# Four of a pair's seven Strassen products in one accumulator, with the partial sums and phi's linear part on ScalarE

## The chip, the cores and the metric

The kernel runs on one core of a Trainium2 chip. The metric is device microseconds of one execution. A core has five engines that run at the same time, each with its own queue of instructions in order: TensorE (PE, matmuls, with weight loads PEld beside it), VectorE (DVE), ScalarE (ACT), GpSimd (POOL) and SyncE (SP, here a queue that issues transfers). Sums of matmuls are formed in PSUM banks of 128x512 fp32; everything else lies in SBUF.

## What is computed

The reference is one transformer block with adaLN conditioning, 2048 rows of 512. Cut to what matters:

```python
phi = lambda t: jnp.where(t > 0, t + 1, jnp.exp(t)) + 1e-6
pq, pk = phi(q), phi(k)                       # 32 heads of 16
kv  = jnp.einsum("bhsd,bhse->bhde", pk, v)
z   = jnp.einsum("bhsd->bhd", pk)
num = jnp.einsum("bhqd,bhde->bhqe", pq, kv)
den = jnp.einsum("bhqd,bhd->bhq", pq, z)[..., None] + 1e-6
o   = num / den                               # then @ wo, gate, residual
...
h   = jnp.einsum("bsd,df->bsf", x, w1) + b1   # x: the normed, modulated rows; 512 -> 1792
act = h * jnp.tanh(softplus(h))               # Mish
y   = jnp.einsum("bsf,fd->bsd", act, w2)      # 1792 -> 512, gate, residual
```

## The kernel before

**Products of fp32 quality.** Every operand is split into a high half (rounded to fp32r) and a low half (what is left). `split` (L71) does this: the high half by a copy on ACT, then, one tick later, the low half by a subtraction on DVE. A product of two split operands is three matmuls (`mm3`, L65): high by high, high by low, low by high. So the third matmul of a group stands on the low half of the operand that is split last.

**Order of the work.** The schedule is written by hand: each engine runs its instructions in the order in which the code emits them. A unit of PE's work is emitted, then work that follows from it is put on a list (`spawn`), and each `tick` lets every generator on the list emit its next step on DVE, ACT or POOL. An instruction whose input isn't ready holds all that is behind it on its engine.

**Stages.** Four blocks of 512 rows go through the layer norm, transposes, then K (`k_unit`, `k_post`), V's part of the sums (`g_unit`), then Q (`q_unit`), the denominators (`den`, L668 on) and the output projection (`o_unit`). `phi` (L239) reads the product in PSUM: Exp on ACT, then on DVE min(e, 1) + 1e-6 and max(p, 0) + that (L243, L244). phi(K) of the four blocks is added into block 0's tiles by DVE (L253) and summed over rows by `z_unit`.

**The feed-forward by Strassen and Winograd.** The first matrix product is taken in 2x2 blocks: a pair g of two column groups of the weights (a11, a12, a22 and sums s1 to s4 of them) and two blocks of rows (b11, b12, b21, b22 and differences t1 to t4). Seven products of 6 matmuls of 128x512 (`product`, L911) and some adds give the four blocks of the result, c11, c12, c21 and c22, each followed by bias and Mish on ACT. There are 7 pairs (G = 7), and all this is done twice: first for row blocks 0 and 1 (loop from L1012), then for blocks 2 and 3 (L1133 on), in the order of pairs 5, 6, 0, 1, 2, 3, 4.

- `pair_begin` (L924): the product a11 b11 and its copy u1 by ACT (L927). The first two pairs are begun early.
- `pair_unit` (L935): s2 t2 is added to u1 on DVE (u2), s3 t3 to that (u3), s1 t1 to u3 (c22), a22 t4 to u3 (all by `add`, L922), a12 b21 is chained by PE onto the bank of a11 b11 (`pair_first`) and s4 b22 onto the bank of s1 t1; the latter with u2 gives c12.
- `mish` (L884) leaves a result that is split at once for the second matrix product; `mish_b` (L905) keeps it for later.
- `trail` and `d_unit` (L891): the second matrix product of one column group of the first row block, 12 matmuls of 128x512. In the first half two of these trailing units stand behind each pair, those of the pair before it. `norm_tile` puts the layer norm of later rows (row sums L210 and L211, apply L198) beside it, `rows` and `w2_job` put the preparation of the next pair's weights (L586 to L589, L513).
- `second` (L962) does the second product of block 1 after all seven pairs.
- In the last half the second matrix product is by Strassen too: `e_unit` does its products m1 and m2 of a pair (12 matmuls of 128x256 each), one pair late; m4, m6, m7, m5 and m3 follow when all pairs are done. `left_trail` prepares their operands on DVE (L1070 to L1074).

PSUM has three kinds of banks: 4 of "acc" (sums of the second product), 3 of "h" and 1 of "tp". SBUF tiles of 128x512 come from one ring of 101.

Of the kernel before, what the change touches and what calls it, by code (L numbers as in the profile page):

```python
# [13 lines left out]
P = 128  # L14
S = 2048
# [10 lines left out]
def block_kernel(ctx: ExitStack, tc: tile.TileContext, x, wqkv, wo, w1, b1t, w2, c, wmodt, out):  # L26
# [18 lines left out]
    def f32(t):  # L45
        return t.bitcast(F32)
# [21 lines left out]
        pe.matmul(o, st[0], mv[1], start=False, stop=False)  # L68
        pe.matmul(o, st[1], mv[0], start=False, stop=stop)  # L69

    def split(name, t, keep, key, lo_engine=dve, hi_engine=act):  # L71

        hi, lo = sb(f"{name}h", F32R, t.shape), sb(f"{name}l", F32R, t.shape)
        if hi_engine is act:
            act.activation(hi, t, AF.Copy)
        else:
            hi_engine.tensor_copy(hi, t)
        if lo_engine is dve:
            yield
        lo_engine.tensor_tensor(lo, t, f32(hi), op=ALU.subtract)  # L80
        keep[key] = hi, lo


# [153 lines left out]
    ku, pk, pq, qs, ms = {}, {}, {}, {}, {}  # L237

    def phi(p, name, dst):  # L239
        e = sb(f"e_{name}")  # L240
        act.activation(e, p, AF.Exp)  # L241
        yield
        dve.tensor_scalar(e, e, 1.0, TINY, op0=ALU.min, op1=ALU.add)  # L243
        dve.scalar_tensor_tensor(dst, p, 0.0, e, op0=ALU.max, op1=ALU.add)  # L244

    def k_post(p, b, t, hi_engine=act):
        u = ku[b, t] = sb(f"ku_{b}_{t}")
        yield from phi(p, f"k_{b}_{t}", u)
        yield from split(f"pk_{b}_{t}", u, pk, (b, t), hi_engine=hi_engine)
        if b:  # L250
            if b < NB - 1:
                yield
            dve.tensor_tensor(ku[0, t], ku[0, t], ku.pop((b, t)), op=ALU.add)  # L253

    def k_unit(b, t):
        p = ps("h", f"pk_{b}_{t}")
# [19 lines left out]
    def z_unit():  # L276

        p = ps("h", "z")
        for t in range(4):
            pe.matmul(p[32 * t:32 * (t + 1), :], ones[:, 0:32], ku.pop((0, t)), start=True, stop=True)  # L280
        act.activation(zsum[0], p, AF.Copy)
        dve.tensor_tensor(zsum[1], p, f32(zsum[0]), op=ALU.subtract)

    def q_unit(b, g):
        p = ps("h", f"pq_{b}_{g}")
# [188 lines left out]
            yield  # L474

    zc = cst.tile([P, 4], F32, name="zc")
    zs = {}

    def z_side():

        zbc_ps = ps("tp", "zbc")
        for i in range(2):
            pe.matmul(zbc_ps, w32, zsum[i], start=i == 0, stop=i == 1)
        zbc = sb("zbc_sb")
        act.activation(zbc, zbc_ps, AF.Copy)
        yield
        for g in range(4):
            diag = cst.tile([P, P], F32, tag="diag", name=f"diag_{g}", bufs=1)
            dve.scalar_tensor_tensor(diag, zbc[:, P * g:P * (g + 1)], 1.0, ident, op0=ALU.mult, op1=ALU.mult,
                                     accum_out=zc[:, g:g + 1])  # L490
            dve.tensor_scalar(hmask[:, g, :], hmask[:, g, :], zc[:, g:g + 1], 1.0, op0=ALU.mult, op1=ALU.mult)
        for k in range(4):
            zs[k] = sb(f"zs_{k}")
            dve.tensor_scalar(zs[k], zbc, mc[:, k:k + 1], 1.0, op0=ALU.mult, op1=ALU.mult)


    w2s, w2d, w2f, op_a = {}, {}, {}, {}
# [171 lines left out]
    def attend(b, wait, queue=pool):  # L669

        p = ps("tp", f"den_{b}")[:, 0:P]
        for g in range(4):
            for t in range(4):
                pe.matmul(p[32 * t:32 * (t + 1), :], hmask[:, g, :], pq[b, g][:, P * t:P * (t + 1)],
                          start=g == 0, stop=g == 3)
        yield
        rden = cst.tile([P, P], F32, tag="rden", name=f"rden_{b}", bufs=2)
        dve.tensor_scalar(rden, p, TINY, 1.0, op0=ALU.add, op1=ALU.mult)
# [101 lines left out]
    def columns(c0, c, done):  # L780

        b11, b12, b21, b22 = [hf.pop((b, c + h)) for h in (0, 2) for b in (c0, c0 + 1)]
        t = [sb(f"t_{c0}_{c}_{i}") for i in range(4)]
        for d, u, v in (t[0], b12, b11), (t[1], b22, t[0]), (t[2], b22, b12), (t[3], b21, t[1]):
            dve.tensor_tensor(d, u, v, op=ALU.subtract)
        yield
        names = [("b11", b11), ("t2", t[1]), ("t3", t[2]), ("t1", t[0]), ("b22", b22), ("t4", t[3]), ("b21", b21)]
# [133 lines left out]
    def add(out, p, u):  # L921
        dve.tensor_tensor(out, p, u, op=ALU.add)  # L922

    def pair_begin(g, tag):  # L924

        u1, p = sb(f"u1_{g}"), product(g, "a11", "b11", tag)
        act.activation(u1, p, AF.Copy)  # L927
        return u1, p

    def pair_first(c0, g, p):  # L930
        m = mish(product(g, "a12", "b21", onto=p), c0, 2 * g)
        next(m)
        spawn(m)

    def pair_unit(c0, g, u1=None, tags=("tp", "h")):  # L935

        f = 2 * g
        u2, u3, c12, c22 = [sb(f"{n}_{g}") for n in ("u2", "u3", "c12", "c22")]
        p11 = None
        if u1 is None:  # L940
            u1, p11 = pair_begin(g, tags[0])
        add(u2, product(g, "s2", "t2"), u1)
        add(u3, product(g, "s3", "t3", tags[1]), u2)
        tick()
        p = product(g, "s1", "t1")
        add(c22, p, u3)
        mish_b(c22, f + 1)
        add(u3, product(g, "a22", "t4"), u3)
        spawn(mish(u3, c0, f + 1))
        tick()  # L950
        if p11 is not None:
            pair_first(c0, g, p11)
        add(c12, product(g, "s4", "b22", onto=p), u2)
        mish_b(c12, f)
        tick()

    def prep_a(b, f):
# [35 lines left out]
            load_wb(6)  # L993


    begun = [pair_begin(g, "h") for g in range(2)]
    tick()
    for g in range(2):
        pair_first(0, g, begun[g][1])
        tick()  # L1000
    for t in (2, 3):
        o_unit(NB - 1, t, "h")
        tick()
    tiles = [norm_tile(b, t) for b in (2, 3) for t in range(4)]
    def trail(f):
        if tiles and (f == 0 or f % 2):
            spawn(tiles.pop(0))
        d_unit(0, f, f)
        ahead(1, f)
        tick()  # L1010

    for g in range(G + 1):  # L1012
        if g < G:
            for f in (2 * g, 2 * g + 1) if g else ():
                spawn(w2_job(f))
            if g == 0:
                spawn(rows(2, 3))
            if g and tiles:
                spawn(tiles.pop(0))
            pair_unit(0, g, begun[g][0] if g < 2 else None)  # L1020
            if g < G - 2:
                store_rows(g)
            if 0 < g < G - 2:
                spawn(rows(g + 2, 2))
            if g == G - 1:
                for n in range(8):
                    load_back("n", nd, 2 + n // 4, n % 4)
        for f in ((0,), (1,))[g] if g < 2 else (2 * g - 2, 2 * g - 1):
            trail(f)
    second(1, prepare)  # L1030


# [25 lines left out]
    def bank(name, i):  # L1058
        return banks[name][i].rearrange("p (t c) -> p t c", t=2)

    def e_unit(n):
        g = pairs[n]
        for c, name in enumerate(("m1", "m2")):
            seventh(name, "acc", ag[L, 2 * g + c], [w[:, c, :] for w in wb[g]], n, G - 1)

    def left_sums(g):

# [49 lines left out]
    def load_wt(name, g):  # L1117
# [10 lines left out]
        else:  # L1128
            pool.dma_start(v, w2t[g][:, :, SUM[name], :])  # L1129

    for n, g in enumerate(pairs):
        if n < 5:
            if n:  # L1133
# [6 lines left out]
        if n == 6:  # L1140
            for m in pairs[:5]:
                load_wt("m4", m)
        pair_unit(L, g, tags=("h", "tp") if n == 1 else ("tp", "h"))
        if n < EARLY:
            spawn(left_trail(g))
        if n:
            e_unit(n - 1)
            tick()

    names = ["m4", "m6", "m7", "m5", "m3"]  # L1150
    units = [(name, n) for name in names for n in range(G)]
# [5 lines left out]
    for k, (name, n) in enumerate(units[:4 * G]):  # L1157
# [12 lines left out]
            spawn(finish(name))  # L1170
        tick()
        if k == 1:
            e_unit(G - 1)
            spawn(finish("m2"))
            tick()

# [41 lines left out]
```

## Time and profile before

| | |
|---|---|
| median of 3 runs | 499.61 us (499.48 to 499.65) |
| the profiled execution | 499.56 us |
| its span, first to last instruction | 497.9 us |
| matmuls | 2648 |
| instructions of DVE, ACT, POOL | 730, 472, 238 |
| granted TensorE clock, mean | 1.000 |

The difference between the profiled execution and its span, 1.66 us, lies ahead of the first and behind the last instruction. In the page's rows, a group is "line, engine, operation, output<-inputs, shapes, count | busy us in all, mean ns of one | idle time ahead of them and what ended it"; a name without its number stands for all tiles of that kind. PE's matmuls overlap: one of 128x512 is listed with 0.39 us, but the next starts 0.23 us later. Products in the pairs appear with outputs `p_a` and `p_s` (L917), the trailing units as `oacc`, m1 to m7 as `m`.

### The profile page before, as it was taken

To read this page: it belongs to the slowest core of one execution; us is meant where nothing else is said; L and a number is where in the kernel's file an instruction comes from. 1 tells how busy PE (TensorE), PEld (TensorE's weight loads), DVE (VectorE), ACT (ScalarE), POOL (GpSimd) and SP (SyncE) were. 2 spreads that over 40 slices of the span, in tenths; PEclk is the share of its full clock that TensorE was granted. 3 is DMA by queue.
4 is the path that set the end of the run, shared out by engine and by line. 5 is a ranking of instruction groups with operands and counts; after the bars stand their busy time and mean duration, and the time that the engine had idled before them with its cause. 6 is when DMAs were issued, how large, how long until landed. Compare 5 with 4: busy or idle time off the path is not lost.

```text
span 497.9 us, 7665 instructions
## 1 busy us (share of the span) xinstructions
PE 490.8 (99%) x2648; PEld 412.3 (83%) x2648; DVE 377.5 (76%) x730; ACT 264.4 (53%) x472; POOL 137.2 (28%) x238
## 2 busy tenths in 40 slices
PE   7999999999999999999999999999999999999997
PEld 5778888878778888888878888888788888899997
DVE  6889775889997979966776765679876666688671
ACT  6776674533351979637787555187343444469000
POOL 4471000100212323101443312323455131545200
PEclk9999999999999999999999999999999999999999
DMA  8721413381554307497799965999999273789312
GB/s 309 284 84 44 156 34 107 127 276 43 131 150 129 96 27 254 142 344 241 245 332 377 289 185 167 307 356 329 376 326 276 63 191 84 188 195 269 91 43 86
DMA packets 65613, 96.49 MB, mean 194 GB/s; under 512 B 7277, under 2 KB 31733, under 8 KB 65574
## 3 DMA queue, kind: packets, MB, share of 16 engines
q1 hardware_dynamic: 37220, 52.51, 31.8%
q0 software_dynamic: 28208, 43.21, 31.2%
q8 instruction: 21, 0.34, 0.3%
q10 hardware_dynamic: 146, 0.26, 0.1%
q14 instruction: 18, 0.15, 0.1%
HBM read 62.92 MB, written 33.03 MB: 193 GB/s over the span
## 4 chain that ended last, share of the span: by engine, by line
PE 95%; DVE 2%; DMA 1%; ACT 1%; POOL 0%; issue 0%; ACTq 0%
PE p_s L917 15%; PE p_a L917 12%; PE oacc L69 5%; PE oacc L68 5%; PE oacc L67 5%; PE m L69 5%; PE m L68 5%; PE m L67 5%; PE o L67 3%; PE pq L67 3%; PE o L69 3%; PE o L68 3%; PE pq L69 3%; PE pq L68 3%; PE gacc L68 3%; PE gacc L69 3%
## 5 line engine op out<-in xcount | busy, mean ns | idle before, releaser
L909 ACT ACTIVATE ub<-c,b1c 128x512 f32<-128x512 f32 x28 | 20.2, 720 | 55.6 <-DVE c L922 55.0
L922 DVE TENSOR_TENSOR c<-p_s,u 128x512 f32<-128x512 f32 x28 | 19.3, 689 | 25.1 <-PE p_s L917 25.1
L922 DVE TENSOR_TENSOR u<-p_s,u 128x512 f32<-128x512 f32 x28 | 19.4, 692 | 22.0 <-PE p_s L917 15.7
L189 POOL TENSOR_TENSOR rs_n<-rs_n,half 128x1 f32<-128x1 f32 x16 | 10.0, 624 | 40.6 <-DVE rs_n L215 31.0
L1129 POOL DMA_DIRECT2D wt_m<-w2t x20 | 14.0, 702 | 24.6 <-PE p_a L917 11.8
L775 ACT ACTIVATE hf_n<-tp_n,mc 128x512 f32<-128x512 f32 x16 | 11.7, 771 | 16.6 <-PE tp_n L773 16.6
L241 ACT ACTIVATE e_q<-pq 128x512 f32<-128x512 f32 x16 | 9.4, 589 | 19.9 <-PE pq L69 19.9
L927 ACT ACTIVATE u<-p_a 128x512 f32<-128x512 f32 x14 | 8.3, 592 | 21.4 <-PE p_a L917 21.4
L241 ACT ACTIVATE e_k<-pk 128x512 f32<-128x512 f32 x16 | 9.4, 591 | 13.2 <-PE pk L69 13.0
L189 POOL TENSOR_TENSOR rs_x<-rs_x,half 128x1 f32<-128x1 f32 (+1 forms) x10 | 7.1, 717 | 33.0 <-DVE rs_x L184 32.2
L573 POOL DMA_DIRECT2D w2b<-w2d x20 | 10.7, 539 | 18.4 <-DVE a_1l L80 4.9
L243 DVE TENSOR_SCALAR e_k<-e_k 128x512 f32<-128x512 f32 x16 | 6.8, 428 | 10.1 <-ACT e_k L241 9.9
L922 DVE TENSOR_TENSOR u<-p_a,u 128x512 f32<-128x512 f32 x14 | 9.7, 692 | 6.0 <-PE p_a L917 5.3
L681 POOL DMA_DIRECT2D rden_d<-rden x3 | 2.2, 739 | 43.1 <-DVE rden L679 43.1
L198 ACT ACTIVATE x<-x,nb_x,rs_x 128x512 f32<-128x512 f32 x15 | 11.6, 807 | 4.5 <-DVE nb_x L193 3.3
L567 POOL DMA_DIRECT2D wb<-w2d x14 | 9.9, 709 | 11.8 <-PE p_a L917 9.3
L693 DVE TENSOR_TENSOR q<-q,rd 128x512 f32<-128x512 f32 x16 | 10.5, 686 | 2.7 <-DMA rd<-rden_d 2.7
L705 DVE TENSOR_TENSOR r<-o,r 128x512 f32<-128x512 f32 x16 | 10.8, 678 | 1.8 <-PE o L69 1.8
L244 DVE SCALAR_TENSOR_TENSOR ku<-pk,e_k 128x512 f32<-128x512 f32 x16 | 11.1, 692 | 0.7
L244 DVE SCALAR_TENSOR_TENSOR q<-pq,e_q 128x512 f32<-128x512 f32 x16 | 11.1, 692 | 0.7
L886 ACT ACTIVATE u<-u,b1c 128x512 f32<-128x512 f32 x14 | 10.0, 715 | 2.8 <-DVE u L922 2.6
L180 DVE BATCH_NORM_STATS2 st_x<-x 128x6 f32<-128x512 f32 x13 | 8.9, 683 | 3.0 <-DMA x<-in_x_dram 3.0
(1328 smaller groups left out, 1921.8 us busy)
## 6 DMA issues: line engine op xcount, KB each, us to landing
wm<-in_wmodt_dram SPq DMA_DIRECT2D x24, 256.0 KB, 5.0
w2b<-w2d POOLq DMA_DIRECT2D x20, 256.0 KB, 6.2
wt_m<-w2t POOLq DMA_DIRECT2D x20, 256.0 KB, 4.1
r<-in_x_dram SPq DMA_DIRECT2D x16, 256.0 KB, 2.8
x<-in_x_dram SPq DMA_DIRECT2D x15, 256.0 KB, 4.8
w1p<-in_w_dram SPq DMA_DIRECT2D x14, 256.0 KB, 4.4
w2r<-in_w_dram SPq DMA_DIRECT2D x14, 256.0 KB, 3.1
wb<-w2d POOLq DMA_DIRECT2D x14, 256.0 KB, 4.6
```

What stands on the lines that cost most here:

```text
L67: pe.matmul(o, st[0], mv[0], start=start, stop=False)
L68: pe.matmul(o, st[0], mv[1], start=False, stop=False)
L69: pe.matmul(o, st[1], mv[0], start=False, stop=stop)
L189: pool.tensor_tensor(y, y, half[:, lo:hi], op=ALU.pow)
L198: act.activation(dst, t, AF.Identity, bias=nb[key, b][:, j:j + 1], scale=rs[key, b][:, j:j + 1])
L241: act.activation(e, p, AF.Exp)
L244: dve.scalar_tensor_tensor(dst, p, 0.0, e, op0=ALU.max, op1=ALU.add)
L775: act.activation(hf[b, j], p, AF.Identity, bias=mc[:, 12 + j:13 + j], scale=mc[:, 16 + j:17 + j])
L909: act.activation(u, p, AF.Mish, bias=b1c[:, f:f + 1])
L917: pe.matmul(p, st, mv, start=onto is None and c == 0 and i == 0, stop=c == 1 and i == 2, skip_group_check=onto is not None)
L922: dve.tensor_tensor(out, p, u, op=ALU.add)
L1129: pool.dma_start(v, w2t[g][:, :, SUM[name], :])
```

## The change

Three things change together.

1. **The pair.** Four products, a11 b11, s2 t2, s3 t3 and a22 t4, are chained by PE in one bank, pa. Between them ACT copies the running sum out: u1 after the first, u2 after the second, u3 after the third; the fourth gives the last block, which Mish reads from the bank. a12 b21 gets a bank of its own, and DVE adds u1 to it (c11). c22 and c12 are added on DVE as before. So per pair there are 3 copies and 3 adds in place of 1 copy and 5 adds. Since a chained product must wait for the copy of what is in its bank, other work is put between: behind s2 t2 the odd trailing unit of the pair before, behind s3 t3 the even one of this pair (`between`), in the last half one m2 unit and one m1 unit. The products' order becomes a11 b11, a12 b21, s1 t1, s2 t2, gap, s3 t3, gap, a22 t4, s4 b22. Unit 13 is left over and follows the last pair.
2. **phi.** ACT does Relu(p) as a second operation, and DVE one operation from SBUF, min(e, 1) + relu. The 1e-6 moves to the operations that follow: the low half of phi(K), the sums z, the denominators (a column `tiny_den`, made once from z) and the product of q with the reciprocal.
3. **phi(K)'s sum.** For blocks 1 and 2 POOL issues a transfer that adds into block 0's tile in place of DVE's add; block 3 stays on DVE.

The core of the diff:

```diff
     def phi(p, name, dst):
-        e = sb(f"e_{name}")
+        e, r = sb(f"e_{name}"), sb(f"relu_{name}")
         act.activation(e, p, AF.Exp)
+        act.activation(r, p, AF.Relu)
         yield
-        dve.tensor_scalar(e, e, 1.0, TINY, op0=ALU.min, op1=ALU.add)
-        dve.scalar_tensor_tensor(dst, p, 0.0, e, op0=ALU.max, op1=ALU.add)
+        dve.scalar_tensor_tensor(dst, e, 1.0, r, op0=ALU.min, op1=ALU.add)
...
-        yield from split(f"pk_{b}_{t}", u, pk, (b, t), hi_engine=hi_engine)
-        if b:
-            if b < NB - 1:
-                yield
+        yield from split(f"pk_{b}_{t}", u, pk, (b, t), hi_engine=hi_engine, plus=TINY)
+        if b == NB - 1:
             dve.tensor_tensor(ku[0, t], ku[0, t], ku.pop((b, t)), op=ALU.add)
+        elif b:
+            pool.dma_start(ku[0, t], ku.pop((b, t)), accum_op=ALU.add)
...
-            dve.tensor_tensor(t, t, rd[g], op=ALU.mult)
+            dve.scalar_tensor_tensor(t, t, TINY, rd[g], op0=ALU.add, op1=ALU.mult)
...
+    def pair_begin(c0, g, tags):
+        u1, pa = sb(f"u1_{g}"), product(g, "a11", "b11", tags[0])
+        act.activation(u1, pa, AF.Copy)
+        c11 = sb(f"c11_{g}")
+        add(c11, product(g, "a12", "b21", tags[1]), u1)
+        return pa, c11
+    def later(p, f, wait=0):
+        for _ in range(wait):
+            yield
+        mish_b(p, f)
+        yield
+    def pair_unit(c0, g, between, begun=None, tags=("tp", "h", "h")):
+        f = 2 * g
+        u2, u3, c12, c22 = [sb(f"{n}_{g}") for n in ("u2", "u3", "c12", "c22")]
+        if begun is None:
+            begun = pair_begin(c0, g, tags)
+            tick()
+        pa, c11 = begun
+        pc = product(g, "s1", "t1", tags[2])
+        product(g, "s2", "t2", onto=pa)
+        act.activation(u2, pa, AF.Copy)
+        spawn(mish(c11, c0, f))
+        tick()
+        between[0]()
+        product(g, "s3", "t3", onto=pa)
+        act.activation(u3, pa, AF.Copy)
+        add(c22, pc, u3)
+        spawn(later(c22, f + 1))
+        between[1]()
+        m = mish(product(g, "a22", "t4", onto=pa), c0, f + 1)
         next(m)
         spawn(m)
...
+        product(g, "s4", "b22", onto=pc)
+        add(c12, pc, u2)
+        spawn(later(c12, f, 1))
         tick()
...
+    begun = {g: pair_begin(0, g, ("tp" if g else "h", "acc")) for g in range(2)}
     tick()
+    o_unit(NB - 1, 2)
+    tick()
...
+    for g in range(G):
+        for f in (2 * g + 2, 2 * g + 3) if g < G - 1 else ():
+            spawn(w2_job(f))
+        if g == 0:
+            spawn(rows(2, 3))
+        if g and tiles:
+            spawn(tiles.pop(0))
+        pair_unit(0, g, (trail(2 * g - 1) if g else last_o, trail(2 * g)), begun.get(g), tags_of(g))
...
+    trail(NF - 1)()
     second(1, prepare)
...
+        pair_unit(L, g, (first, second_gap), begun.pop(n, None), tags_of(n))
         if n < EARLY:
             spawn(left_trail(g))
-        if n:
-            e_unit(n - 1)
-            tick()
```

`last_o` is the last `o_unit` of the attention; `first` begins the second pair of the last half (n = 0) or does m2 of the pair before (n > 0), and `second_gap` does m1 of this pair. The names of the splits of b and t are put into the order in which the products now use them.

More of the change, by code (lines that the diff above doesn't have):

```diff
@@ L69, in mm3, with split @@
         pe.matmul(o, st[1], mv[0], start=False, stop=stop)
-    def split(name, t, keep, key, lo_engine=dve, hi_engine=act):
+    def split(name, t, keep, key, lo_engine=dve, hi_engine=act, plus=None):
         hi, lo = sb(f"{name}h", F32R, t.shape), sb(f"{name}l", F32R, t.shape)
@@ L79, in split @@
             yield
-        lo_engine.tensor_tensor(lo, t, f32(hi), op=ALU.subtract)
+        if plus is None:
+            lo_engine.tensor_tensor(lo, t, f32(hi), op=ALU.subtract)
+        else:
+            dve.scalar_tensor_tensor(lo, t, plus, f32(hi), op0=ALU.add, op1=ALU.subtract)
         keep[key] = hi, lo
@@ L281, in z_unit @@
         act.activation(zsum[0], p, AF.Copy)
-        dve.tensor_tensor(zsum[1], p, f32(zsum[0]), op=ALU.subtract)
+        dve.scalar_tensor_tensor(zsum[1], p, S * TINY / 4, f32(zsum[0]), op0=ALU.add, op1=ALU.subtract)
     def q_unit(b, g):
@@ L476, in block_kernel @@
     zc = cst.tile([P, 4], F32, name="zc")
+    zh = cst.tile([P, 32], F32, name="zh")
+    tiny_den = cst.tile([P, 1], F32, name="tiny_den")
     zs = {}
@@ L494, in z_side @@
             dve.tensor_scalar(zs[k], zbc, mc[:, k:k + 1], 1.0, op0=ALU.mult, op1=ALU.mult)
+        dve.tensor_reduce(zh, zbc.rearrange("p (h r) -> p h r", r=16), op=ALU.add, axis=mybir.AxisListType.X)
+        diag = cst.tile([P, P], F32, tag="diag", name="diag_den", bufs=1)
+        dve.scalar_tensor_tensor(diag.rearrange("p (t h) -> p t h", t=4), ident.rearrange("p (t h) -> p t h", t=4),
+                                 TINY, zh.unsqueeze(1).to_broadcast([P, 4, 32]), op0=ALU.mult, op1=ALU.mult,
+                                 accum_out=tiny_den)
+        dve.tensor_scalar(tiny_den, tiny_den, TINY, 1.0, op0=ALU.add, op1=ALU.mult)
     w2s, w2d, w2f, op_a = {}, {}, {}, {}
@@ L677, in attend @@
         rden = cst.tile([P, P], F32, tag="rden", name=f"rden_{b}", bufs=2)
-        dve.tensor_scalar(rden, p, TINY, 1.0, op0=ALU.add, op1=ALU.mult)
+        dve.tensor_scalar(rden, p, tiny_den[:, 0:1], 1.0, op0=ALU.add, op1=ALU.mult)
         dve.reciprocal(rden, rden)
@@ L786, in columns @@
         yield
-        names = [("b11", b11), ("t2", t[1]), ("t3", t[2]), ("t1", t[0]), ("b22", b22), ("t4", t[3]), ("b21", b21)]
+        names = [("b11", b11), ("b21", b21), ("t1", t[0]), ("t2", t[1]), ("t3", t[2]), ("t4", t[3]), ("b22", b22)]
         halves = [split(f"{name}_{c0}_{c}", v, op_b, (name, c)) for name, v in names if name not in done]
@@ L922, in add @@
         dve.tensor_tensor(out, p, u, op=ALU.add)
[L924 to L931, printed above, removed]
+    def pair_begin(c0, g, tags):
[28 more added lines that the diff above has]
+        m = mish(product(g, "a22", "t4", onto=pa), c0, f + 1)
         next(m)
         spawn(m)
[L935 to L943, printed above, removed]
-        tick()
[L945 to L954, printed above, removed]
+        product(g, "s4", "b22", onto=pc)
+        add(c12, pc, u2)
+        spawn(later(c12, f, 1))
         tick()
@@ L993, in prepare, with tags_of, unit, last_o @@
             load_wb(6)
-    begun = [pair_begin(g, "h") for g in range(2)]
+    def tags_of(n):
+        return "tp" if n % 2 else "h", "h", "h"
+    begun = {g: pair_begin(0, g, ("tp" if g else "h", "acc")) for g in range(2)}
     tick()
[L998 to L1003, printed above, removed]
+    o_unit(NB - 1, 2)
+    tick()
     tiles = [norm_tile(b, t) for b in (2, 3) for t in range(4)]
     def trail(f):
-        if tiles and (f == 0 or f % 2):
-            spawn(tiles.pop(0))
[L1008 to L1029, printed above, removed]
+        def unit():
+            if tiles and (f == 0 or f % 2):
+                spawn(tiles.pop(0))
+            d_unit(0, f, f)
+            ahead(1, f)
+            tick()
+        return unit
+    def last_o():
+        o_unit(NB - 1, 3)
+        tick()
+    for g in range(G):
[4 more added lines that the diff above has]
+        if g and tiles:
+            spawn(tiles.pop(0))
+        pair_unit(0, g, (trail(2 * g - 1) if g else last_o, trail(2 * g)), begun.get(g), tags_of(g))
+        if g < G - 2:
+            store_rows(g)
+        if 0 < g < G - 2:
+            spawn(rows(g + 2, 2))
+        if g == G - 1:
+            for n in range(8):
+                load_back("n", nd, 2 + n // 4, n % 4)
+    trail(NF - 1)()
     second(1, prepare)
@@ L1059, in bank, with e_unit @@
         return banks[name][i].rearrange("p (t c) -> p t c", t=2)
-    def e_unit(n):
+    def e_unit(c, n):
         g = pairs[n]
-        for c, name in enumerate(("m1", "m2")):
-            seventh(name, "acc", ag[L, 2 * g + c], [w[:, c, :] for w in wb[g]], n, G - 1)
+        seventh(("m1", "m2")[c], "acc", ag[L, 2 * g + c], [w[:, c, :] for w in wb[g]], n, G - 1)
     def left_sums(g):
@@ L1129, in load_wt, with begin_next @@
             pool.dma_start(v, w2t[g][:, :, SUM[name], :])
+    begun = {}
+    def begin_next():
+        begun[1] = pair_begin(L, pairs[1], ("tp", "acc"))
     for n, g in enumerate(pairs):
@@ L1142, in block_kernel, with first, second_gap @@
                 load_wt("m4", m)
-        pair_unit(L, g, tags=("h", "tp") if n == 1 else ("tp", "h"))
+        def first(n=n):
+            if n == 0:
+                begin_next()
+            else:
+                e_unit(1, n - 1)
+            tick()
+        def second_gap(n=n):
+            e_unit(0, n)
+            tick()
+        pair_unit(L, g, (first, second_gap), begun.pop(n, None), tags_of(n))
         if n < EARLY:
             spawn(left_trail(g))
-        if n:
-            e_unit(n - 1)
-            tick()
     names = ["m4", "m6", "m7", "m5", "m3"]
@@ L1172, in block_kernel @@
         if k == 1:
-            e_unit(G - 1)
+            e_unit(1, G - 1)
             spawn(finish("m2"))
```

## The prediction

> **What bounds the kernel now.** The page comes first: how busy each engine is, the slices, the chain, and the groups that the change touches.
>
> ```profile
> PE 490.8 (99%) x2648; PEld 412.3 (83%) x2648; DVE 377.5 (76%) x730; ACT 264.4 (53%) x472; POOL 137.2 (28%) x238
> ...
> PEclk9999999999999999999999999999999999999999
> ...
> PE 95%; DVE 2%; DMA 1%; ACT 1%; POOL 0%; issue 0%; ACTq 0%
> ...
> L909 ACT ACTIVATE ub<-c,b1c 128x512 f32<-128x512 f32 x28 | 20.2, 720 | 55.6 <-DVE c L922 55.0
> L922 DVE TENSOR_TENSOR c<-p_s,u 128x512 f32<-128x512 f32 x28 | 19.3, 689 | 25.1 <-PE p_s L917 25.1
> ...
> L927 ACT ACTIVATE u<-p_a 128x512 f32<-128x512 f32 x14 | 8.3, 592 | 21.4 <-PE p_a L917 21.4
> L241 ACT ACTIVATE e_k<-pk 128x512 f32<-128x512 f32 x16 | 9.4, 591 | 13.2 <-PE pk L69 13.0
> ...
> L243 DVE TENSOR_SCALAR e_k<-e_k 128x512 f32<-128x512 f32 x16 | 6.8, 428 | 10.1 <-ACT e_k L241 9.9
> ...
> w2b<-w2d POOLq DMA_DIRECT2D x20, 256.0 KB, 6.2
> ```
>
> TensorE (PE) is busy for 490.8 of 497.9 us, its clock is full in every slice, and it holds 95% of the chain. VectorE (DVE) and ScalarE (ACT) have room on average. So what DVE loses is worth nothing by itself, and whatever delays one matmul is paid in full. Next, PE's own waits:
>
> ```profile
> PE warm L126 <- POOL ones L120: 1.1, 1, 1.1
> PE tp_x L374 <- ACT x L198: 1.0, 3, 0.4
> PE sc_bc L132 <- ACT c L130: 0.7, 1, 0.7
> PE pk L418 <- ACT hT_x_0h L399: 0.4, 1, 0.4
> PE gacc L68 <- DVE pk_0l L80: 0.2, 1, 0.2
> PE gacc L68 <- DVE rs_x L215: 0.2, 1, 0.2
> ```
>
> Together 3.6 us, all in the front; none is at a product (L917). What is left to win in the pairs shows in the chain, whose pieces are start, length and matmuls:
>
> ```profile
> 239.15 3.02 PE p_a L917 x12
> ...
> 248.97 1.55 PE p_a L917 x6
> ...
> 254.62 2.76 PE p_a L917 x12
> 257.37 1.59 PE p_s L917 x6
> ...
> 269.87 2.72 PE p_a L917 x12
> 272.59 1.36 PE p_s L917 x6
> ...
> 365.03 1.63 PE p_s L917 x6
> ```
>
> Undisturbed, 12 matmuls of 128x512 take 2.72 us and one product (6) takes 1.36, 0.227 each. The other pieces run over by 0.30, 0.19, 0.04, 0.23 and 0.27: **1.0 us** is all that the pairs lose today.
>
> **How I price a handover.** The timeline of PE, then of ACT, then of DVE (start, duration):
>
> ```profile
> 23.56 0.50 PE L68 MATMUL gacc<-pk_0l,xn_0h 128*128 128x512 f32 x1 [0.23 <-DVE pk_0l L80]
> 23.90 0.40 PE L69 MATMUL gacc<-pk_0h,xn_0l 128*128 128x512 f32 x1
> ...
> 380.05 0.39 PE L917 MATMUL p_a<-b_1h,a1b 128*128 128x512 f32 x1
> 380.28 0.39 PE L917 MATMUL p_s<-t_0h,s12b 128*128 128x512 f32 x1
> ...
> 388.21 0.39 PE L917 MATMUL p_s<-b_1h,s34b 128*128 128x512 f32 x1
> 388.44 0.28 PE L67 MATMUL m<-wb,a_12h 128*128 128x256 f32 x1
> 388.55 0.28 PE L68 MATMUL m<-wb,a_12h 128*128 128x256 f32 x1
> ```
>
> ```profile
> 222.86 0.62 ACT L210 ACTIVATE scrap_n<-r 128x512 f32<-128x512 f32 x1
> ...
> 224.32 0.62 ACT L75 ACTIVATE a_2h<-w1p 128x512 fp32r<-128x512 f32 x1
> 224.84 0.62 ACT L75 ACTIVATE s_2h<-s 128x512 fp32r<-128x512 f32 x1
> ...
> 380.48 0.60 ACT L927 ACTIVATE u<-p_a 128x512 f32<-128x512 f32 x1 [2.29 <-PE p_a L917]
> ...
> 387.00 0.71 ACT L886 ACTIVATE u<-u,b1c 128x512 f32<-128x512 f32 x1
> 387.74 0.63 ACT L75 ACTIVATE a_1h<-u 128x512 fp32r<-128x512 f32 x1
> ```
>
> ```profile
> 22.81 0.69 DVE L80 TENSOR_TENSOR pk_0l<-ku,pk_0h 128x512 fp32r<-128x512 f32 x1
> ...
> 388.64 0.69 DVE L922 TENSOR_TENSOR c<-p_s,u 128x512 f32<-128x512 f32 x1 [2.03 <-PE p_s L917]
> 389.25 0.68 DVE L80 TENSOR_TENSOR l_6l<-ub,l_6h 128x512 fp32r<-128x512 f32 x1
> ```
>
> Where a product's last matmul ends its slot (380.28, 388.44), ACT or DVE starts reading 0.20 later. DVE starts its next 128x512 operation 0.61 after the last. ACT needs 0.52 from copy to copy, 0.74 from Mish to the high half of its result, and 1.46 (222.86 to 224.32) for a tile's row sums. DVE's result is used by PE 0.06 after its end (23.50 to 23.56), and the matmul behind such a wait follows after 0.34 instead of 0.227: each stall costs 0.11 more. A 128x256 matmul takes 0.12.
>
> **The change part by part.** PE issues the same matmuls, so their 490.8 us stay. DVE loses 28 adds of 689 ns and phi's 32 operations of some 428; ACT gains 28 copies at L927's 592 and 32 Relus, which no row shows: I take the Exp's 591. As totals, ACT goes from 264.4 to 264.4 + 28 x 0.592 + 32 x 0.591 = 300 us and DVE to about 345, both covered by PE. What counts is the order of each queue. In the new order a pair runs on PE as A (a11 b11), B (a12 b21), C (s1 t1), D (s2 t2 on A's bank), a gap filled with the trailing unit (12 matmuls), E (s3 t3), a second gap, F (a22 t4), G (s4 b22 on C's bank). Then the next A follows at once; before, the two trailing units stood there. I walk the queues with G's or D's end as zero.
>
> *Copies of sums.* E waits for the copy u2: ready 0.20 + 0.60 after D, behind it a gap of 2.72 us. F waits for u3 in the same way. Cost 0 while ACT comes to the copy at once; without the gap it would be 0.8 per copy.
>
> *Boundary between pairs, 2 to 6 (**+4.9**).* A's third matmul needs the low half a1l. DVE makes it behind the add c12, which waits for G. c12 starts at 0.20, a1l at 0.81 and ends at 1.50, PE goes on at 1.56; it would have been there at 2 x 0.227 = 0.45. That is 1.11 + 0.11 = 1.22 at each of the four boundaries from pair 2 to pair 6 (pair 2's own a1l is made early). Before, 5.4 us of trailing matmuls lay over this add. Bounds: 0 if a1l is made ahead of c12, 1.9 if one more DVE operation slips between.
>
> *Trailing unit 13 (**+1.8**).* It stands alone after the last G of the first half. DVE has c12, a_1_11l and then a_0_13l: 0.20 + 2 x 0.61 + 0.69 = 2.11, PE at 2.17 instead of 0.45, with the restart 1.8. Bounds 1.2 to 2.
>
> *First pair, C (**+1.1**).* From B's end of the second begun pair, one o unit (2.72) covers DVE's c11_1 and six operations up to the low half of t1's second part: start 0.20 + 6 x 0.61 = 3.86, PE 4.61. C's fifth matmul would be at 2.72 + 4 x 0.227 = 3.63. So 0.98 + 0.11. Before, t1 was the fourth product and not the third.
>
> *Pair 1, second gap (**+2.3**).* Unit 2 stands on a_0_2h, and ACT has after D: u2, two weights' high halves, the layer norm's apply (its bias column comes from DVE at about 1.75), Mish ub_0, row sums, Mish of c11_1, a_0_2h. The groups price the apply:
>
> ```profile
> L198 ACT ACTIVATE r<-r,nb_n,rs_n 128x512 f32<-128x512 f32 x8 | 6.5, 807 | 2.8 <-DVE nb_n L219 2.8
> ```
>
> 0.20 + 3 x 0.52 = 1.76, apply and Mish to 3.2, sums to 4.65, Mish to 5.39, a_0_2h to 6.02, PE 6.08, against 2.72 + 1.36 = 4.08: 2.0 + 0.11; the low half is another 0.2 late. Bounds 1 (if the sums go ahead of D) to 3.
>
> *Pair 2, D (**+1.1**).* D goes onto A's bank and so waits for the copy u1. With G1's end as zero, ACT does two applies (0.75 each from start to start), two Mishes (0.63 and 0.74), three high halves (1.6) and u1 (0.60) from about 0.1 on: 5.2, against A to C, 4.08. Bounds 0.5 to 1.3.
>
> *Last half, first pair (**+1.7**).* The unit that now sits in its second gap needs a_2_10l. DVE is at c11_5 at 2.92 after the pair's start, makes two low halves and four 128x256 sums (0.38 each) to 6.3; ACT then t1_4h, Mish of c11_5, its high half and u1_6 to 8.7; DVE c11_6, two low halves, a_2_10l to 11.3. PE would be there after seven products and two matmuls of 128x256, at 9.76: 1.57 + 0.11. Bounds 0.8 to 2.1.
>
> *Last half, second pair (**+0.6**).* From D: u2, Mish ub_10, Mish of c11_6, high half, low half: 0.20 + 0.52 + 0.63 + 0.74 + 0.66 + 0.69 = 3.44, PE 3.50, against 1.44 + 1.36 + 0.24 = 3.04. Without the extra Mish, in pairs 2 to 6, it is 2.87: nothing, by a margin of 0.2.
>
> *phi (**+0.2**).* Exp and Relu of the next tile stand ahead of the first high half pk_0h, some 0.45 later at a unit that PE waits for today (23.56); most of it is taken up again by the next wait. DVE's chain loses 0.43 there, so the bounds are -0.6 and +0.6. Later tiles have 2.72 us of matmuls each over 1.1 us on ACT: 0.
>
> *ku by adding transfers (0).* Nothing here shows an accumulating transfer; the nearest row, a 256 KB transfer of POOL's queue, lands after 6.2 us, and the last is issued a block of four k units (10.9 us) ahead of its reader. Bounds 0 and, if it takes twice as long, some 2.
>
> *Removed (**-1.0**)*: the overruns above go.
>
> Sum: 4.9 + 1.8 + 1.1 + 2.3 + 1.1 + 1.7 + 0.6 + 0.2 - 1.0 = **+12.7 us**. The profiled execution took 499.56 us (span 497.9 and 1.66 around it), 0.05 below the median of 499.61: 499.56 + 12.7 = **512.3 us**.
>
> **A rule of the skill beside it.** The Trainium skill, "Perfetto Trace Analysis", section Optimizing Scalar/DVE Operations, says that where DVE is saturated, offloading work to Scalar may make sense. At 76% busy with PE at 99% this trace has nothing that the rule could win; by it alone the sum would be the -1.0 only, which is the rival Faster below.
>
> **Rivals.**
> - *Covered* (about 499.6). Copies and adds all fit into the gaps, and the removed 1.0 pays for a few small waits. For it: every gap is 2.72 us and a copy 0.59. Against it: c12, a1l and A are in one line, and no gap is between them. It needs a boundary cost below 0.2.
> - *Faster* (about 498). One mechanism: with 28 adds fewer DVE reaches its low halves earlier, so the 1.0 of overruns and part of the front's waits at pk (0.2 and 0.2, and the restarts) go, -1.5 in all. It decides if DVE makes a1l before G ends, that is, if the tick that issues it comes before the add. In the order it comes after, so I give it little.
> - *ACT bound* (about 519). A pair takes 7 x 1.36 + 2 x 2.72 = 15.0 us of PE, and ACT has up to 12.7 us in it (three copies 1.6, four Mishes 2.6, eight high halves 4.2, the sums and applies of up to two tiles 4.3). If each E or F of the first half waits 0.5 for its copy, 14 waits add 7 us to the forecast: 519. For it: pair 1's stall. Against it: from pair 3 on the copy's turn comes 1 to 2 us ahead of need. A stall near 3.4 us would do the same in another way: the matmuls after it would run slower. By the Trainium skill, "TensorE: Matmul & The Clock Gate", section Part 1, an idle window of about 3.4 us brings the half clock back; no run here shows it, since the granted clock is full throughout and no wait here is over 1.1 us.
> - *Boundary alone* (about 505). Only the DVE lines hold, 4.9 + 1.8, less 1.0, and ACT's waits dissolve: 505.3. Within the forecast's range.
>
> **How the numbers follow.** Slower by 4 to 18 us, forecast and boundary alone together: 0.80. ACT bound, above 518: 0.04. Slower by less than 4: 0.03. Covered: 0.05. Faster: 0.08. About 0.2% (1 us) is what a measurement can tell from no change. So slower 0.87, same 0.05, faster 0.08. The range goes from 503.5 (the boundary terms less all gains) to 518 (all terms at their upper bounds: 7.6 + 2 + 1.1 + 3 + 1.3 + 2.1 + 0.6 + 0.6 = 18.3).
>
> **What would show it.** PE waiting for a1l (L80) at each pair's third matmul, about 1.1 us four times, and then the restart of 0.34; a wait on a_0_2h of about 2 us in pair 1, on a_0_13l of 1.7; PE's busy time unchanged and its waits 15 us and more. If A follows G without a gap, the largest term is wrong. If the copies u2 and u3 are what PE waits for, ACT is the bound. If the waits lie in the front, phi is.

## The result and the profile after

The changed kernel takes **513.35 us** (median of 4 runs, 513.23 to 514.83), the kernel before 499.63 us (499.48 to 499.83): ratio 1.028, 95% interval 1.026 to 1.030, so 13.7 us slower. 512.3 was forecast. The profiled execution took 513.23 us, 13.67 above that of before.

The page of the changed kernel, the rows that answer to those of before:

```profile
PE 493.9 (97%) x2648; PEld 412.1 (81%) x2648; DVE 344.2 (67%) x666; ACT 295.0 (58%) x532; POOL 145.1 (28%) x246
...
PEclk9999999999999999999999999999999999999999
...
PE 81%; ACT 6%; DVE 4%; issue 4%; DMA 2%; POOL 1%; DVEq 0%; POOLq 0%; ACTq 0%
...
L967 ACT ACTIVATE u<-p_a 128x512 f32<-128x512 f32 x14 | 8.3, 594 | 10.1 <-PE p_a L930 10.1
```

PE still has 2648 matmuls and is listed with 3.1 us more busy time: a matmul behind a wait is listed longer (0.50 instead of 0.39), and each wait breaks the overlap with the one before. DVE is at 344 us, as counted (about 345), and ACT at 295, 5 under the count of 300: its 60 new operations cost 0.51 each, ACT's spacing from start to start, and not their listed 0.59. The chain lies on PE for 81% of the span instead of 95%. Where it goes, PE's waits tell (us in total, times, longest):

```profile
PE m L69 <- DVE a_10l L81: 1.8, 1, 1.8
PE oacc L67 <- ACT a_2h L75: 1.7, 1, 1.7
...
PE oacc L69 <- DVE a_13l L81: 1.2, 1, 1.2
...
PE p_a L930 <- DVE a_3l L81: 0.9, 1, 0.9
PE p_a L930 <- DVE a_4l L81: 0.9, 1, 0.9
PE p_a L930 <- DVE a_5l L81: 0.9, 1, 0.9
PE p_a L930 <- DVE a_6l L81: 0.9, 1, 0.9
PE p_s L930 <- DVE t_1l L81: 0.8, 1, 0.8
PE m L69 <- DVE l_m_5l L81: 0.7, 1, 0.7
PE p_a L930 <- ACT u L940: 0.5, 1, 0.5
...
PE m L69 <- DVE a_12l L81: 0.2, 1, 0.2
```

These 11 waits are all new and all behind 200 us: 10.5 us together. How much more than its listed idle time a wait costs is to be seen at one of them, the boundary to pair 3, in PE's timeline:

```profile
255.26 0.39 PE L930 MATMUL p_s<-b_3h,s_2l 128*128 128x512 f32 x1
255.49 0.39 PE L930 MATMUL p_a<-b_0h,a_3h 128*128 128x512 f32 x1
255.72 0.39 PE L930 MATMUL p_a<-b_0l,a_3h 128*128 128x512 f32 x1
257.03 0.50 PE L930 MATMUL p_a<-b_0h,a_3l 128*128 128x512 f32 x1 [0.93 <-DVE a_3l L81]
257.37 0.39 PE L930 MATMUL p_a<-b_1h,a_3h 128*128 128x512 f32 x1
```

From start to start 257.03 - 255.72 = 1.31 instead of 0.23: 1.08 lost, of which the row shows 0.93 as idle (the rest is the pipelined tail of the matmul before). The next start is 0.34 later, another 0.11. So a wait costs about 0.27 more than its row says, and the 11 waits cost 10.5 + 11 x 0.27 = **13.5 us**, nearly all of the 13.67. DVE's timeline at the same place:

```profile
255.69 0.69 DVE L935 TENSOR_TENSOR c<-p_s,u 128x512 f32<-128x512 f32 x1 [2.43 <-PE p_s L930]
256.30 0.68 DVE L81 TENSOR_TENSOR a_3l<-w1p,a_3h 128x512 fp32r<-128x512 f32 x1
```

DVE had been idle for 2.43 us, with a_3l's inputs long there, because the add of c12 ahead of it waited for the last product (255.26, slot end 255.49, add 255.69). That is the forecast's largest term as it was written. The second kind of wait is one on ACT's order, in pair 1:

```profile
229.35 0.80 ACT L201 ACTIVATE r<-r,nb_n,rs_n 128x512 f32<-128x512 f32 x1
230.05 0.71 ACT L922 ACTIVATE ub<-c,b1c 128x512 f32<-128x512 f32 x1
230.66 0.62 ACT L213 ACTIVATE scrap_n<-r 128x512 f32<-128x512 f32 x1
...
232.13 0.71 ACT L899 ACTIVATE u<-c,b1c 128x512 f32<-128x512 f32 x1
232.87 0.63 ACT L75 ACTIVATE a_2h<-u 128x512 fp32r<-128x512 f32 x1
```

```profile
231.50 0.39 PE L930 MATMUL p_a<-t_1h,s_1l 128*128 128x512 f32 x1
233.55 0.50 PE L67 MATMUL oacc<-w_2h,a_2h 128*128 128x512 f32 x1 [1.66 <-ACT a_2h L75]
```

The upper fence is ACT, the lower PE: PE was done with the bank's third product (s3 t3) at 231.73, and ACT, with the apply, a Mish and the row sums ahead, had the high half a_2h 1.8 us after that.

### The profile page after: what moved, and what is told of

It reads as the page before. It is cut to its first block, busy times and chain, and to the rows that moved or that the text cites. A ratio compares the mean times of both kernels' runs of the same rounds, so it can differ in the third digit from the quotient of the medians.

```text
span 511.4 us, 7692 instructions
## 1 busy us (share of the span) xinstructions
PE 493.9 (97%) x2648; PEld 412.1 (81%) x2648; DVE 344.2 (67%) x666; ACT 295.0 (58%) x532; POOL 145.1 (28%) x246
## 4 chain that ended last, share of the span: by engine, by line
PE 81%; ACT 6%; DVE 4%; issue 4%; DMA 2%; POOL 1%; DVEq 0%; POOLq 0%; ACTq 0%
PE p_a L930 15%; PE p_s L930 6%; PE oacc L69 4%; PE oacc L68 4%; PE oacc L67 4%; PE m L69 4%; PE m L68 3%; PE m L67 3%; PE pq L67 3%; PE gacc L68 3%; PE gacc L69 3%; PE gacc L67 3%; PE pq L69 3%; PE pq L68 3%; PE o L67 3%
## 5 line engine op out<-in xcount | busy, mean ns | idle before, releaser
L962 ACT ACTIVATE u<-p_a 128x512 f32<-128x512 f32 x14 | 8.4, 597 | 32.5 <-PE p_a L930 32.3
L248 DVE SCALAR_TENSOR_TENSOR ku<-e_k,relu_k 128x512 f32<-128x512 f32 x16 | 11.0, 689 | 14.5 <-ACT relu_k L246 14.5
L940 ACT ACTIVATE u<-p_a 128x512 f32<-128x512 f32 x14 | 8.3, 593 | 15.6 <-PE p_a L930 15.6
L935 DVE TENSOR_TENSOR c<-p_a,u 128x512 f32<-128x512 f32 x14 | 9.7, 690 | 8.6 <-ACT u L940 5.8
L899 ACT ACTIVATE u<-p_a,b1c 128x512 f32<-128x512 f32 x14 | 9.6, 686 | 10.1 <-PE p_a L930 8.5
L248 DVE SCALAR_TENSOR_TENSOR q<-e_q,relu_q 128x512 f32<-128x512 f32 x16 | 11.0, 688 | 4.7 <-ACT relu_q L246 4.5
L967 ACT ACTIVATE u<-p_a 128x512 f32<-128x512 f32 x14 | 8.3, 594 | 10.1 <-PE p_a L930 10.1
L201 ACT ACTIVATE r<-r,nb_n,rs_n 128x512 f32<-128x512 f32 x8 | 6.5, 812 | 10.7 <-DVE nb_n L222 8.9
L706 DVE SCALAR_TENSOR_TENSOR q<-q,rd 128x512 f32<-128x512 f32 x16 | 10.6, 686 | 2.6 <-DMA rd<-rden_d 2.5
```

What stands on the lines that cost most here:

```text
L201: act.activation(dst, t, AF.Identity, bias=nb[key, b][:, j:j + 1], scale=rs[key, b][:, j:j + 1])
L248: dve.scalar_tensor_tensor(dst, e, 1.0, r, op0=ALU.min, op1=ALU.add)
```

## The experiments

The theory: every engine keeps the order in which the code emits; the change took the trailing units away from the places where they covered DVE and ACT, so a few low and high halves come late, and the sum of these waits is the loss. The rivals: ScalarE is the bound (its 28 copies and 32 Relus), the chained bank costs something by itself, or phi or the transfers have a share.

**The pair alone, phi as before** (`phi`, `k_post`, `z_unit`, `den` and the product with the reciprocal taken from the kernel before).

```diff
     def phi(p, name, dst):
...
-        act.activation(r, p, AF.Relu)
...
-        dve.scalar_tensor_tensor(dst, e, 1.0, r, op0=ALU.min, op1=ALU.add)
...
+        dve.tensor_scalar(e, e, 1.0, TINY, op0=ALU.min, op1=ALU.add)
+        dve.scalar_tensor_tensor(dst, p, 0.0, e, op0=ALU.max, op1=ALU.add)
```

> The changed kernel with phi, its 1e-6 and the sum of phi(K) as they were before; only the pair's order is changed. Queue order (theory): all the loss behind 200 us stays, only the front's 0.3 us goes: 513.0 to 513.2, 13.4 us over the kernel before. Rival, phi has a share by its load on ScalarE or by the ring of tiles: 511 or less.

Measured: 513.76 us (513.41 to 514.82), 1.029 of before (1.028 to 1.031). The whole loss is the pair's. The median lies 0.6 above the expected 513.0 to 513.2; the one execution with a mean clock of 0.999 took 513.41, the three with 0.996 or 0.997 took 513.68 to 514.82 (the last section has more on that). All eleven waits are in its trace with the times that they have in the changed kernel's; only the front's differ a little.

**phi alone, the pair as before** (the reverse).

> The kernel before with phi's linear part on ScalarE and phi(K)'s sum by adding transfers, the pair as it was. Queue order: 0.3 us slower than before (499.9), the front's waits alone. Rival, DVE freed by 32 operations helps: 499.0 or less. Rival, the new transfers collide with others: 501 or more.

Measured: 499.96 us (499.23 to 500.49, 11 runs) against 499.61; ratio 1.0005, interval 0.9996 to 1.0014. Neither rival holds, and whether phi costs 0.3 us or nothing can't be told: its runs spread over 1.3 us, those of before over 0.4. What spreads them stays open.

**The add of c12 behind the low halves** (`sum_later` does the add as its first step and Mish a tick later).

```diff
-        add(c12, pc, u2)
-        spawn(later(c12, f, 1))
+        spawn(sum_later(c12, pc, u2, f))
         tick()
```

> The changed kernel, with the add of c12 emitted at the end of the tick, behind the low halves. Nothing else moves. Queue order: the four boundaries between pairs lose their 1.20 us each (4.8), the unit after the last pair about 1.0 of its 1.8; pair 1, pair 2 and the last half keep theirs: 507.4 (507 to 508). Rival, ScalarE is what bounds the pairs: the waits move to its copies or high halves and at most 2 us are won: 511 or more.

Measured: 508.61 us (507.88 to 509.43), 1.018 of before; 4.7 us won. PE's waits in its trace:

```profile
PE m L69 <- DVE a_10l L81: 1.8, 1, 1.8
PE oacc L67 <- ACT a_2h L75: 1.7, 1, 1.7
PE m L69 <- DVE l_m_5l L81: 1.3, 1, 1.3
...
PE p_s L930 <- DVE t_1l L81: 0.8, 1, 0.8
```

The four waits of the boundaries and a_13l are gone, as the theory had it; nothing took their place on ACT. The wait on the copy u1 in pair 2 is missing too, which was not expected. That 1.2 us less was won than expected has two main reasons. l_m_5l went from 0.7 to 1.3: c12's add, now behind the low half, comes 0.6 later in the last half too, and DVE's work behind it with it. And in this execution PE ran at half its clock behind pair 1's wait. The windows view, the columns being the stretch, its length, five engines' busy time (count), the granted clock, DMA share and GB/s:

```profile
230.00:234.00 4.00, 2.79 (x13) 1.98 (x11) 1.34 (x3) 3.94 (x9) 2.02 (x4) 1.00 1.03 286
234.00:236.00 2.00, 1.51 (x5) 0.99 (x6) 0.69 (x1) 1.97 (x6) 0.00 (x0) 0.95 0.89 261
236.00:239.00 3.00, 3.00 (x8) 2.32 (x8) 1.76 (x4) 1.21 (x3) 0.00 (x0) 0.50 0.96 346
239.00:242.00 3.00, 3.00 (x14) 2.43 (x14) 1.36 (x5) 1.82 (x3) 1.13 (x2) 0.96 1.05 403
```

For 3 us matmuls start every 0.43 us. The four executions had mean clocks of 0.997, 0.997, 1.000 and 0.996 and took 509.03, 508.20, 507.88 and 509.43: the one at full clock is 0.5 from the expectation.

**The copies u2 and u3 done twice** (28 more copies).

```diff
         act.activation(u2, pa, AF.Copy)
+        act.activation(u2, pa, AF.Copy)
...
+        act.activation(u3, pa, AF.Copy)
```

> The changed kernel with each of the copies u2 and u3 done twice, 28 copies of 0.59 us more on ScalarE. ScalarE bound: each copy is paid, 28 x 0.52 = 14.6 us, 526 or more. Copies fully covered: 0. Queue order: nothing in pairs 3 to 6, where the first half's high halves have some 0.9 us of margin, but about 0.5 where ScalarE's queue is late already (pair 1, pair 2, the last half's second pair) and some 0.45 at each of the last half's later pairs, whose margin is 0.2: 3 to 5 us in all, 516.5 to 518.5.

Measured: 518.92 us (518.75 to 519.01), 5.6 over the changed kernel, a little above the expected 3 to 5. Its trace shows where:

```profile
PE m L69 <- DVE a_10l L81: 2.4, 1, 2.4
PE oacc L67 <- ACT a_2h L75: 2.3, 1, 2.3
...
PE p_a L930 <- DVE a_3l L81: 0.9, 1, 0.9
...
PE p_a L930 <- ACT u L940: 0.8, 1, 0.8
```

Two of ACT's places, pair 1 and the last half's first pair, got 0.6 worse each (that the latter, a_10l, is one of them was missed), the wait on u1 0.3, and the boundaries stayed at 0.9. Nearly half of the 5.6 us is in gaps that are too short for this list, at the last half's five later pairs:

```profile
404.40 0.28 PE L68 MATMUL m<-wb,a_0h 128*128 128x256 f32 x1
404.79 0.39 PE L69 MATMUL m<-wb,a_0l 128*128 128x256 f32 x1
405.02 0.28 PE L67 MATMUL m<-wb,a_0h 128*128 128x256 f32 x1
```

These two steps, 0.39 and 0.23 from start to start, are about 0.12 each in the changed kernel, and from one such pair to the next it is 12.96 us instead of 12.44: 0.5 five times, 2.6 in all, where 0.45 each was expected. ScalarE isn't the bound: 16 us more of its work (310.9 us busy instead of 295.0) cost a third of that, where its queue was late already or had the least margin.

**The layer norm's tile one unit later in pair 1.**

```diff
-        if g and tiles:
+        if g > 1 and tiles:
             spawn(tiles.pop(0))
```

> The changed kernel, with the layer norm of one tile started one trailing unit later in pair 1, so that its row sums no longer stand ahead of the high half a_0_2h on ScalarE. Queue order: the wait in pair 1 falls from 2.2 us to about 1.0, that of pair 2's fourth product on the copy u1 (0.8) goes, the rest stays: 511.3 (511.0 to 511.8), and no wait is long enough for the half clock, if that comes from pair 1's wait: the times lie closer together than 0.5 us. Rival, the wait in pair 1 is one on transfers or on the weights: no change, 513.3.

Measured: 511.86 us (510.76 to 512.96). The profiled execution took 511.39, with a_2h's wait at 0.2 instead of 1.7 (about 1.0 was expected) and the wait on u1 gone; t_1l's in the first pair, which wasn't touched, was 1.3 instead of 0.8 in it. The median is within the expectation but for 0.1. The expectation on the half clock failed: the executions at 510.76 and 511.39 had a clock of 1.000, those at 512.34 and 512.96 had 0.996 and 0.997. The two slower ones have no trace. If pair 1's wait was as short in them, it isn't the only one that the half clock can follow, and a_10l's 1.8 is still there; which it was isn't shown.

**Two other orders mended**: the adds of c11 of the two begun pairs are emitted after the next `o_unit`, and in the last half one tick stands ahead of the second pair's beginning.

```diff
             if n == 0:
+                tick()
                 begin_next()
```

> The changed kernel with two orders mended: in the first pair of all, the two adds of c11 are emitted after the splits of t1; in the last half's first pair, one more step of the waiting generators is emitted ahead of the second pair's beginning, so that the low half a_2_10l stands ahead of the add of c11. Queue order: 1.1 and 2.0 us go, the rest stays: 510.2 (509.9 to 511.5 with the half clock). Rival, the products there wait for ScalarE's high halves: at most 1 us is won, 512.3 or more.

Measured: 510.38 us (510.11 to 510.70), 3.0 won of the 3.1 expected; the waits on t_1l and a_10l are gone and all others are as they were.

**All orders mended.** The three edits above, c12 late only in the first half, and the two below. `EARLY` is the number of pairs whose left operands are prepared ahead of the tail, the stretch behind the last pair.

```diff
-            spawn(later(c12, f, 1))
+            spawn(later(c12, f, 1 if g == 4 else 2))
...
-    pairs, EARLY = [5, 6, 0, 1, 2, 3, 4], 5
+    pairs, EARLY = [5, 6, 0, 1, 2, 3, 4], 6
```

> The changed kernel with all orders mended: c12 behind the low halves in the first half, the tile's layer norm later, c11 and a_2_10l as in the run before, Mish of c12 one step later in the last half, and the operands of m4 of one more pair prepared ahead of the tail. Queue order: of 14.7 us behind 200 us some 2.2 stay (pair 1 1.0, unit 13 0.6, two of 0.25): 500.8 (500.4 to 501.5). Rival, there is a cost of the chained bank itself (ScalarE's copy holding up PE, or more load on ScalarE): 503 or more.

Measured: 502.51 us (502.13 to 503.13), 1.7 above the expectation. Not by the bank: its trace has five new waits, of which one row stands for all,

```profile
PE m L69 <- DVE a_4l L81: 0.2, 1, 0.2
```

each 0.2 + 0.27, 2.4 in all. Mish of c12, put off by one tick, now stood ahead of the next pair's Mish in the pairs where it hadn't before. An edit that was right for one pair was wrong for five.

**Nothing between the chained products** (the trailing units of pairs 1 to 6 emitted behind the pair, ACT's and DVE's order kept; `held` is run behind `pair_unit`, units 0 and 13 stay where they are).

```diff
-            d_unit(0, f, f)
+            if f == 0 or f == NF - 1:
+                d_unit(0, f, f)
+            else:
+                held.append(lambda: d_unit(0, f, f))
             ahead(1, f)
             tick()
```

> The changed kernel, with the trailing units of pairs 1 to 6 in the first half put behind the pair as they were before, while ScalarE's and DVE's order stays: nothing lies between a chained product and the copy ahead of it. Queue order: each of the two copies costs 0.20 + 0.60 + 0.06 + 0.11 = 0.97 us in pairs 4 to 6 (5.8 in all), more in pairs 2 and 3 (3.6 each) and 1 (7.7), where row sums stand ahead of u3; the boundaries' 4.8, unit 13's 1.8, pair 1's 2.2 and pair 2's 0.8 go: about 11 us slower than the changed kernel, 524 (519 to 528). Rival, PE goes on without waiting for the copy, or the gaps were not needed: 505 or less.

Measured: 529.54 and 531.81 us, 17 over the changed kernel where 11 were expected, and above the expected 519 to 528. The first two rows of PE's waits:

```profile
PE p_a L930 <- ACT u L967: 13.9, 6, 6.2
PE p_a L930 <- ACT u L962: 4.1, 6, 0.7
```

A product that is chained behind its copy with nothing between waits 0.7 by the row, 0.97 with what the wait adds: the forecast's "0.8 per copy" and the restart. u3 waits longer where row sums stand ahead of it (13.9 over 6). Most of what is missing to 17 is the half clock again (mean 0.986 and 0.987; the late starts add up to some 4.9 us in the trace): after 6.2 us of waiting PE's next starts are 0.43 apart for 3.4 us.

```profile
236.29 0.80 PE L930 MATMUL p_a<-t_0h,a_1h 128*128 128x512 f32 x1 [6.20 <-ACT u L967]
236.88 0.63 PE L930 MATMUL p_a<-t_0l,a_1h 128*128 128x512 f32 x1
237.31 0.63 PE L930 MATMUL p_a<-t_0h,a_1l 128*128 128x512 f32 x1
```

**The mended version corrected, with the new phi and with the old.** Mish of c12 one tick later in the last half's first pair alone (`2 if g == 5 else 1`), and the first layer norm tile a unit later as well (`if tiles and f % 2`).

> The run e7_all with two orders corrected: Mish of c12 comes one step later in the last half's first pair alone (in e7_all its place in the later pairs gave five new waits of 0.48 us), and the layer norm's first tile too starts one trailing unit later, out of pair 1's way. Queue order: of e7_all's waits behind 200 us (4.1 us) only unit 13's 0.6 and one of 0.3 stay, about as much as the kernel before loses there (1.1): 499.6 (499.3 to 500.3), no measurable difference from before. Rival, the chained bank or ScalarE's load costs something by itself: 501 or more.

> The same with phi and the sum of phi(K) as before. Queue order: the front's 0.3 us go as well: 499.4 (499.1 to 499.9); a gain over the kernel before of 0.2 us at most, since only its own 1.1 us of lost time in the pairs can be won. Rival, phi's form on ScalarE helps where the chain leaves it room: slower than e9_mended.

Measured: 499.44 us (499.00 to 500.18; ratio 0.9999, 0.9990 to 1.0008) with the new phi, 499.43 us (499.29 to 499.61; 0.9997, 0.9988 to 1.0006) with the old, against 499.56. All 13.7 us are gone, with the four chained products and the ScalarE copies still there; the version with the new phi has as many instructions on every engine as the changed kernel. PE's waits with the new phi, all of them:

```profile
PE warm L129 <- POOL ones L123: 1.1, 1, 1.1
PE tp_x L378 <- ACT x L201: 0.9, 3, 0.4
PE pk L422 <- ACT hT_x_0h L403: 0.4, 1, 0.4
PE sc_bc L135 <- ACT c L133: 0.4, 1, 0.4
PE tp_x L230 <- ACT x L201: 0.2, 1, 0.2
PE gacc L68 <- DVE pk_0l L83: 0.2, 1, 0.2
```

3.2 us, all in the front, as before (3.6). Neither version is faster than the kernel before by more than can be measured: only about 1 us was there to win.

## Why the prediction was right, point by point

| step | forecast, us | measured, us |
|---|---|---|
| boundaries to pairs 3 to 6 | +4.9 | 4 x (0.9 + 0.27) = 4.7 |
| trailing unit 13 | +1.8 | 1.2 + 0.27 = 1.5, and 0.3 by its first matmul, late on the high half |
| first pair, third product | +1.1 | 0.8 + 0.27 = 1.1 |
| pair 1, second gap | +2.3 | 1.7 + 0.27 = 2.0, and 0.3 by the low half |
| pair 2, fourth product | +1.1 | 0.5 + 0.27 = 0.8 |
| last half, first pair | +1.7 | 1.8 + 0.27 = 2.1 |
| last half, second pair | +0.6 | 0.2 + 0.27 = 0.5 |
| phi | +0.2 | 0.3 in the run with phi alone (interval -0.2 to 0.7); -0.3 between the two traces |
| overruns removed | -1.0 | -0.6: those at the products went, one of 0.24 at a trailing unit (a_4l) is new |
| tail, l_m_5l | 0 | 0.7 + 0.27 = 1.0 |

The sum of the column is 14.0 with phi's 0.3, and 13.4 with the -0.3 that the two traces show (the pairs' first product starts at 203.36 us instead of 203.63); between the two profiled executions it is 13.67, between their spans 13.5. So phi's cost is too small for either way to tell, and its sign stays open. The adding transfers, put at 0, land after 4.2 us in the median (8 of 256 KB), and PE has no wait on a transfer. The likeliest case came out, by its own mechanism and at its places. The method was to walk each queue at the handovers with spacings from the timelines, and for the four boundaries it gave 1.22 where the trace has 1.19. The mended kernels show that these are causes and not marks: the orders put right took their own rows out of the waits (those of a_12l and l_m_5l only together with the others), and with all of them right the whole loss was gone.

Two sizes were off that came to little. The overruns were read from the chain as 1.0; from start to start the timeline of before has 0.8 at the products. And PE's busy time was to stay and its waits to come to 15 us or more: it is 3.1 us higher, and the rows of all its waits, the front's included, come to 13.8, because the list books some 0.27 of each wait as busy time. The misses at phi, the overruns, pair 2 and the last half's first pair, 0.3 to 0.5 each, nearly cancel; that only the tail is left of the difference is in part luck.

Missed was one step, the tail: the forecast walked the pairs and left the stretch behind them at nothing. There DVE has the left operands of two pairs and four adds ahead of l_m_5l:

```profile
465.55 1.47 DVE L1113 TENSOR_TENSOR rq<-rq,m 128x512 f32<-128x512 f32 x2
466.94 0.68 DVE L81 TENSOR_TENSOR l_m_5l<-u,l_m_5h 128x512 fp32r<-128x512 f32 x1
```

DVE is busy without a break there, and one unit (m1 of the last pair, 1.44 us) that had covered this work now stands in the last pair's gap. The mended kernels, which prepare one more pair's operands earlier, don't have this wait; that edit wasn't run alone.

Of the rivals, Covered fails at the point it named: c12, a1l and the next product are in one line and no gap is between them. Faster fails since DVE made a1l after the add, as the code emits it. ACT bound fails by the doubled copies. Boundary alone was too small: ACT's late places and the last half's first pair held as well.

The Trainium skill, "Perfetto Trace Analysis", section Optimizing Scalar/DVE Operations, names a saturated DVE as the case in which moving work to Scalar may make sense. Here DVE was 76% busy before and 67% after, and the mended kernel with DVE at 344 us instead of 378 is no faster: the trace agrees.

## What to carry to other kernels

With an engine at 99%, moving work between the others can't win more than that engine's own waits; count those first, here 1 us in the stage that was changed. When units of the bound engine are moved to cover one thing, ask what they covered where they stood: here an add that waits for the last product had two units over it, and without them it held up the low half behind it. Such waits are mended by the order of emission, and each mend has to be walked through every pass of the loop, not only the one that showed the wait.

## What the runs showed of the hardware that was not expected

After a wait of PE, its granted clock can fall to one half for some 3 us. After 1.7 us of idle time it did so in one profiled execution (0.50 from 236 to 239 us in the run with c12 late, where PE had started again at 234.5), but not in the profiled execution of the changed kernel, with the same wait; there one of the four executions had a mean clock of 0.997 and took 514.83 us, 1.4 to 1.6 more than the three at 0.999 or 1.000. One spell of 3.4 us at half the clock takes 0.003 off the mean over 512 us; so 0.997 or 0.996 is read here as such a spell where there is no trace. Executions read so took 0.3 to 2.2 us more than the fastest one of the same kernel. In the run without gaps, three waits of 2.3, 3.1 and 6.2 us were each followed by it. In the run with the copies doubled, waits of 2.3 and 2.4 us were not: its four executions had mean clocks of 0.999 or 1.000 and lie within 0.3 us. So a wait can cost more than its length, but the length alone doesn't decide it, and some of the kernels with long waits spread over up to 2.3 us, where the kernel before spread over 0.4 to 0.7. The Trainium skill, "TensorE: Matmul & The Clock Gate", section Part 1, gives an idle window of about 3.4 us for the fall to half clock, and calls the window free-running. That the clock halves, and that the same wait does it in one execution and not in another, agrees with the runs; that waits of half that length can be enough is not what the page leads one to expect.
